# One set of expert weight buffers up to tile 63 and two from tile 64 on, where it was two from tile 34 on

## The chip, the cores and the metric

The kernel runs on one core of one Trainium2 chip. The metric is the device time of one execution in microseconds (us). TensorE (PE) multiplies, VectorE (DVE), ScalarE (ACT) and GpSimd (POOL) do the rest, and SyncE (SP) issues nearly all DMA transfers, in the order of its own queue.

## The reference

Eight sequences of 5696 tokens with 128 features are convolved along the sequence with one filter, and each token then goes through one of eight experts.

```
Xf = np.fft.rfft(x, n=2*S, axis=1); Hf = np.fft.rfft(h, n=2*S, axis=0)
y = np.fft.irfft(Xf * Hf[None], n=2*S, axis=1)[:, :S, :]
logits = y @ w_gate                      # 45568 tokens, 8 experts
expert_idx = argmax(logits); gate_w = softmax(logits)[expert_idx]
for e in range(8):                       # w1: 128x1024, w2: 1024x128
    out[mask_e] = gate_w * (relu(y[mask_e] @ w1[e]) @ w2[e])
```

## The kernel before

The convolution is three stages of matrix products over frequencies: A (lines 305 to 400, `pa`), B (`phase_b`, `xp` and `vp`) and C (`phase_c`, `yp`, which also makes the logits and scatters each token's row into `SR`, sorted by expert). The eight sequences go through them in three groups of 2, 3 and 3. While group 1 is in stage C, group 2's stage A runs beside it, and then group 2's stage B alone.

The experts are worked off in tiles of 256 sorted tokens, 185 in all. Each tile reads its first row and its expert from a small table (`tables`, line 1183). The tiles come in four parts, each of which is sorted by expert from the start: tiles 0 to 25, 26 to 58, 59 to 103 and 104 to 184. `pipeline` (line 1507) places the tiles between the work of the convolution. A tile has four steps k = 0 to 3. In step k, `layer1` makes two blocks of 128 hidden features (`mh`, lines 1375 to 1379), `relu` leaves them in `hs`, and `layer2` adds them up (`ma`, lines 1417 to 1422) two steps later. So layer 2 of a tile's steps 2 and 3 runs beside the next tile's steps 0 and 1. Up to tile 21 the tiles use plain weights; from tile 22 on, weights and activations are split into two parts and each product takes three passes.

A set of split weights is four buffers of 512 KB, `wb{z}_{n}`. Chunk n = 0 serves layer 1 of steps 0 and 1, chunk 1 of steps 2 and 3, chunks 2 and 3 serve layer 2 likewise. `load_w(t, n)` (line 1320) issues the load of chunk n of tile t from `WD`. The load carries a flag from the table: where it is 0, the transfer is skipped, as the buffer already holds that expert. It is not conditional for the first `sets(t)` tiles of a part (one, or two from part 2 on), and for two tiles that are named.

`home(t)` says which set a tile uses. It is the same set for all tiles below `LONE`, and from there on the sets 0 and 1 take turns. `user[t]` is the tile that used the set of tile t last. `pipeline` places the load of chunk n only when that tile's last step with chunk n has been placed (lines 1517 to 1524):

```
while nw[0] < min(t + 3, hi) and known(nw[0]) and (not nw[0] or state["brief"] > 3):
    was, n = user[nw[0]], nw[1]
    ...
    if was is not None and was >= lo and passed.get((was, n // 2), -1) < 2 * (n % 2) + 1:
        break
    load_w(nw[0], n)
```

SP waits at such a load until TensorE has done that step, and everything behind it in SP's queue waits as well: token rows (`xr`), matrices (`mt`), filter (`hh`) and input (`uq`) of stage B, and its output (`VU<-vt`). The table's flag compares a tile's expert with that of the tile before (`back` 1) as long as there is one set, and with that of two tiles before (`back` 2) where there are two (lines 1254 to 1258).

Of the kernel before, what the change touches and what calls it, by code (L numbers as in the profile page):

```python
# [59 lines left out]
KNOWN = (0, 2840, 2840)  # L60
STAGED = 64
PAIRED = 2
LONE = 34
HEAD = (0, 8, 2)
REST = (4, 1, 4)
FRONT = (1, 8, 2)
# [24 lines left out]
def conv_moe(ctx: ExitStack, tc: tile.TileContext, I, out, B, S, D, E, F, split):  # L91
# [1091 lines left out]
    def tables(pt, base):  # L1183
# [69 lines left out]
        nc.vector.memset(tab[:, 2, :], 1)  # L1253
        alone = min(max(LONE + 2 - sum(p.nt for p in parts[:g]), 0), NT)
        for back, lo, hi in ((1, 1, alone), (2, max(2, alone), NT)):
# [42 lines left out]
    def sets(t):  # L1298
        return 2 if seq[t][0].s >= PAIRED else 1

    def home(t):
        return (t - LONE) % 2 if t >= LONE else 0

# [16 lines left out]
    def load_w(t, n):  # L1320
        pt, j = seq[t]
        z, fixed = home(t), j < sets(t) or t in (PLAIN, LONE + 1)
        if n == 0:
# [417 lines left out]
```

## Time and profile before

| what | value |
|---|---|
| time, median of 3 runs (lowest, highest) | 2053.92 us (2049.94, 2055.18) |
| the profiled execution: its own time, span | 2054.73 us, 2053.1 us |
| TensorE busy in the span | 1975.3 us (96%) |
| DVE, ACT, POOL busy | 68%, 49%, 59% |
| weight loads `wb<-WD` on SP, moved and skipped together | 640, 512 KB each |

The span is from the first instruction to the last; the execution's own time has 1.6 us more around it. A busy share says little by itself here: the stages have different limits, and a wait is read in the stretch in which it stands.

### The profile page before, as it was taken

The numbers are of one execution on the slowest core, as the hardware profiler recorded it, in microseconds if no ns is written. First come the engines' busy times: TensorE is split into PE (matmuls) and PEld (weight loads), VectorE is DVE, ScalarE is ACT, GpSimd is POOL, SyncE is SP. The second block draws the span as 40 slices with busy tenths as digits, with TensorE's granted clock in tenths as the row PEclk, the third lists the DMA queues.
The fourth block names the chain that finished last, engine by engine and source line by source line (L and its number), as shares of the span: only waits on it lengthen the run. The fifth ranks groups of instructions, "written<-read, shape, count | busy, mean of one in ns | idle before, by whom it ended". The sixth has DMA issues, their size and how long they took to land.

```text
span 2053.1 us, 46737 instructions
## 1 busy us (share of the span) xinstructions
PE 1975.3 (96%) x14480; PEld 1517.0 (74%) x14480; DVE 1394.1 (68%) x3116; ACT 1014.6 (49%) x2219; POOL 1208.7 (59%) x1367
## 2 busy tenths in 40 slices
PE   9999898999999898989999999999999999999998
PEld 5788454555556565666766678888899999999997
DVE  6788676345644688767777666888866666666665
ACT  4788453344434454534444444444445555555554
POOL 2356177656653388885666661888875444444433
PEclk9999999999999999989999999999999999999999
DMA  9899997999998878789999987767654444443331
GB/s 361 265 295 316 320 383 289 245 278 334 303 305 296 292 265 316 254 235 289 306 296 315 297 253 250 238 202 247 214 170 156 147 148 144 149 133 122 114 102 35
DMA packets 263787, 496.80 MB, mean 242 GB/s; under 512 B 32946, under 2 KB 168887, under 8 KB 263536
## 3 DMA queue, kind: packets, MB, share of 16 engines
q1 hardware_dynamic: 239168, 445.48, 68.8%
q0 software_dynamic: 24368, 48.29, 7.1%
q8 instruction: 118, 1.93, 0.4%
q14 instruction: 133, 1.09, 0.2%
HBM read 558.54 MB, written 191.22 MB: 365 GB/s over the span
## 4 chain that ended last, share of the span: by engine, by line
PE 61%; DMA 7%; issue 4%; POOL 3%; DVE 1%; SPq 1%; ACT 1%; POOLq 0%; DVEq 0%; ACTq 0%
PE mh L1379 20%; PE ma L1422 9%; PE ma L1419 6%; PE xp L595 6%; PE ma L1417 3%; PE mx L213 3%; PE yp L896 3%; DMA wb<-WD 2%; PE mh L1376 2%; PE ma L1409 2%; PE pa L341 2%; DMA wf<-moe_w 2%; PE tp L213 2%; PE vp L666 2%; POOL SR L800 1%
## 5 line engine op out<-in xcount | busy, mean ns | idle before, releaser
L1392 DVE SCALAR_TENSOR_TENSOR hs<-mh,hs 128x512 fp32r<-128x512 f32 x640 | 440.7, 689 | 326.8 <-ACT hs L1390 326.5
L1379 PE MATMUL mh<-xtb,wb 128*128 128x256 f32 x3840 | 591.8, 290 | 15.4 <-DMA wb<-WD 10.8
L1379 PEld LDWEIGHTS mh<-xtb,wb 128*128 128x128 f32 x3840 | 519.0, 190 | 113.5 <-issue 40.0
L1390 ACT ACTIVATE hs<-mh 128x512 fp32r<-128x512 f32 x640 | 381.7, 596 | 369.2 <-PE mh L1379 346.3
L800 POOL DMA_INDIRECT SR<-rt,pi x384 | 398.1, 1037 | 217.8 <-issue 43.5
L1483 POOL DMA_INDIRECT out<-xr x264 | 258.8, 980 | 329.5 <-DVE xr L1446 277.0
L1422 PE MATMUL ma<-hs,wb 128*128 128x256 f32 x1848 | 279.6, 288 | 2.9 <-DMA wb<-WD 2.9
L705 ACT COPY vt<-vp 128x384 f32<-128x384 f32 (+1 forms) x300 | 149.9, 500 | 237.4 <-PE vp L666 226.0
L1419 PE MATMUL ma<-hs,wb 128*128 128x512 f32 x664 | 259.8, 408 | 0.0
L1422 PEld LDWEIGHTS ma<-hs,wb 128*128 128x128 f32 x1848 | 244.3, 193 | 3.7 <-DMA wb<-WD 3.5
L595 PE MATMUL xp<-uq,mt 48*64 48x384 f32 x960 | 200.8, 510 | 4.9 <-DMA uq<-VU 4.7
L666 PE MATMUL vp<-zt,mt 48*64 48x384 f32 x960 | 200.6, 509 | 0.0
L1417 PE MATMUL ma<-hs,wb 128*128 128x256 f32 x664 | 173.5, 282 | 0.0
L1483 POOL DMA_INDIRECT out<-xb x100 | 97.9, 979 | 121.6 <-ACT hs L1390 96.2
L640 DVE TENSOR_TENSOR zt<-xp,hh 128x384 f32<-128x384 f32 x240 | 122.3, 551 | 65.3 <-PE vp L666 51.0
L1419 PEld LDWEIGHTS ma<-hs,wb 128*128 128x128 f32 x664 | 125.7, 189 | 10.7 <-DVE hs L1392 0.2
L648 POOL TENSOR_TENSOR zt<-zt,hh 128x384 f32<-128x384 f32 x114 | 113.1, 1023 | 30.0 <-DVE hh L634 29.5
L1417 PEld LDWEIGHTS ma<-hs,wb 128*128 128x128 f32 x664 | 126.6, 191 | 3.5
L648 POOL TENSOR_TENSOR zt<-zt,xs 128x384 f32<-128x384 f32 x116 | 116.1, 1032 | 19.8 <-DVE xs L634 19.3
L794 POOL TENSOR_TENSOR idle_row<-idle_row 128x64 f32<-128x64 f32 (+1 forms) x288 | 117.0, 406 | 2.3
L884 DVE TENSOR_TENSOR vr<-vq 120x384 f32<-120x384 f32 x192 | 108.4, 607 | 0.0
L652 POOL TENSOR_TENSOR zt<-zt,xs 128x512 f32<-128x512 f32 x60 | 76.0, 1276 | 46.6 <-DVE xs L620 30.1
(167 smaller groups left out, 3095.6 us busy)
## 6 DMA issues: line engine op xcount, KB each, us to landing
wb<-WD SPq DMA_DIRECT2D x640, 512.0 KB
vq<-VU SPq DMA_DIRECT2D x124, 384.0 KB
VU<-vt SPq DMA_DIRECT2D x60, 768.0 KB
VU<-ut SPq DMA_DIRECT2D x48, 768.0 KB
uq<-VU SPq DMA_DIRECT2D x120, 288.0 KB
xt<-x SPq DMA_DIRECT2D x96, 256.0 KB
xr<-SR SPq DMA_DIRECT2D x182, 130.0 KB
wf<-moe_w SPq DMA_DIRECT2D x88, 256.0 KB
```

Source lines behind the costliest of these rows:

```text
L595: nc.tensor.matmul(xp[e * HP : (e + 1) * HP, :cw], lhs, uq[at, j], start=True, stop=True)
L648: eng.tensor_tensor(out=zt, in0=zt, in1=xs, op=ALU.add)
L666: nc.tensor.matmul(vp[to, :cw], mt[at, lo : lo + HP], zj, start=True, stop=True)
L705: nc.scalar.copy(dst, banks.pop(n)[:upto, : QW * cw].rearrange("p (j x) -> p j x", x=cw))
L800: s = nc.gpsimd.indirect_dma_start(out=SR[:, :], out_offset=IndirectOffsetOnAxis(ap=pi[:, b : b + 1], axis=0), in_=rt[:, b, :], in_offset= ...
L1379: nc.tensor.matmul(hp[:, u, :], wb[:, a, f, :], xt[:, b, :], start=(n == 0), stop=(n == 2))
L1390: done = nc.scalar.activation(hs[:, 0], hp, AF.Relu)
L1392: nc.vector.scalar_tensor_tensor(out=hs[:, 1], in0=hp, scalar=0.0, in1=hs[:, 0].bitcast(F32), op0=ALU.max, op1=ALU.subtract)
L1417: nc.tensor.matmul(accs[t][:, 0], wb[:, 1, f, :], hs[:, 0, u, :], start=False, stop=False)
L1419: nc.tensor.matmul(accs[t], wb[:, 0, f, :], hs[:, :, u, :], start=begin, stop=end)
L1422: nc.tensor.matmul(accs[t], wb[:, a, f, :], hs[:, b, u, :], start=(k == 0 and u == 0 and n == 0), stop=(k == NPAIR - 1 and u == 1 and n == 2),
L1483: sc = nc.gpsimd.indirect_dma_start(out=out[:, :], out_offset=IndirectOffsetOnAxis(ap=xr[:, s, D + 1 : D + 2].bitcast(I32), axis=0), in_=x ...
```

## The change

The constant `LONE` is 64 where it was 34. Three lines read it: the table's flags (1254), `home` (1302) and the tile whose load is not conditional because it fills set 1 for the first time (1322; it was tile 35, it is now tile 65).

```
-LONE = 34
+LONE = 64
...
 alone = min(max(LONE + 2 - sum(p.nt for p in parts[:g]), 0), NT)
...
 def home(t):
     return (t - LONE) % 2 if t >= LONE else 0
...
 z, fixed = home(t), j < sets(t) or t in (PLAIN, LONE + 1)
```

The order of all instructions on TensorE, ACT and POOL stays as it was; only the names of the weight buffers change. On DVE the comparisons that make the flags cover other columns of the table. Here is TensorE's queue at the end of tile 37 and the start of tile 38, in the middle of group 2's stage B (`mh37_3` is layer 1 of tile 37's step 3, `ma37` its layer 2, `wb1_1` is chunk 1 of set 1; `mh38_0` is the start of tile 38). Before:

```order
L1379 MATMUL mh37_3_12376<-xtb37_12195,wb1_1_11786 128x256 x6
L1422 MATMUL ma37_12346<-hs37_1_12304,wb1_2_11788 128x256 x6
...
L1379 MATMUL mh38_0_12420<-xtb38_12369,wb0_0_7686 128x256 x6
L1422 MATMUL ma37_12346<-hs37_2_12366,wb1_3_11790 128x256 x6
...
L1379 MATMUL mh38_1_12455<-xtb38_12369,wb0_0_7686 128x256 x6
L1422 MATMUL ma37_12346<-hs37_3_12401,wb1_3_11790 128x256 x6
```

And in the changed kernel:

```order
L1379 MATMUL mh37_3_12359<-xtb37_12178,wb0_1_7688 128x256 x6
L1422 MATMUL ma37_12329<-hs37_1_12287,wb0_2_7690 128x256 x6
...
L1379 MATMUL mh38_0_12403<-xtb38_12352,wb0_0_7686 128x256 x6
L1422 MATMUL ma37_12329<-hs37_2_12349,wb0_3_7692 128x256 x6
...
L1379 MATMUL mh38_1_12438<-xtb38_12352,wb0_0_7686 128x256 x6
L1422 MATMUL ma37_12329<-hs37_3_12384,wb0_3_7692 128x256 x6
```

The rows stand in the same places; tile 37 now reads the buffers that tile 38 reads.

On SP the weight loads keep their places too, but each place now serves one tile earlier. This is SP's queue while TensorE is in tile 36 (`xr40` are tile 40's token rows, the other transfers belong to stage B). Before, where the first row is the last chunk of tile 37 and the next four loads are tile 38's:

```order
L1340 DMA wb1_3_11790<-WD_74 128x1024
...
L1340 DMA wb0_0_7686<-WD_74 128x1024
L692 DMA VU2_72<-vt2_4_11959 128x4x384
...
L1340 DMA wb0_1_7688<-WD_74 128x1024
...
L1340 DMA wb0_2_7690<-WD_74 128x1024
...
L1313 DMA xr40_12244<-SR_69 128x260
L512 DMA mt2_28_12259<-mm 128x400
L541 DMA hh1_98<-HS_73 128x512
L530 DMA uq2_28_12262<-VU2_72 48x4x384 x2
...
L1340 DMA wb0_3_7692<-WD_74 128x1024
```

And in the changed kernel, where the first row is the last chunk of tile 36 and the next four loads are tile 37's:

```order
L1340 DMA wb0_3_7692<-WD_74 128x1024
...
L1340 DMA wb0_0_7686<-WD_74 128x1024
L692 DMA VU2_72<-vt2_4_11942 128x4x384
...
L1340 DMA wb0_1_7688<-WD_74 128x1024
...
L1340 DMA wb0_2_7690<-WD_74 128x1024
...
L1313 DMA xr40_12227<-SR_69 128x260
L512 DMA mt2_28_12242<-mm 128x400
L541 DMA hh1_98<-HS_73 128x512
L530 DMA uq2_28_12245<-VU2_72 48x4x384 x2
...
L1340 DMA wb0_3_7692<-WD_74 128x1024
```

The four loads of a tile are now issued while the tile directly before it is worked on, where it was the tile before that one. At the end of the changed stretch the shift of one tile is made up for. While TensorE is in tiles 63 and 64, SP's queue was, with the last chunk of tile 65 and then tile 66's first:

```order
L1313 DMA xr67_16843<-SR_69 128x260
...
L1340 DMA wb1_3_11790<-WD_74 128x1024
L1324 TENSOR_LOAD tab2_11702
...
L1325 TENSOR_LOAD tab2_11702
...
L1340 DMA wb0_0_7686<-WD_74 128x1024
L692 DMA VU2_72<-vt2_116_16743 128x4x384
```

In the changed kernel the first load here is the last chunk of tile 64, all four chunks of tile 65 follow, and then tile 66's first:

```order
L1313 DMA xr67_16826<-SR_69 128x260
...
L1340 DMA wb0_3_7692<-WD_74 128x1024
L1324 TENSOR_LOAD tab2_11701
...
L1340 DMA wb1_0_16876<-WD_74 128x1024
...
L1340 DMA wb1_1_16878<-WD_74 128x1024
...
L1340 DMA wb1_2_16880<-WD_74 128x1024
...
L1340 DMA wb1_3_16882<-WD_74 128x1024
L1324 TENSOR_LOAD tab2_11701
...
L1340 DMA wb0_0_7686<-WD_74 128x1024
L692 DMA VU2_72<-vt2_116_16726 128x4x384
```

Four loads that stood behind tile 34's before (tile 35's, the first filling of set 1) stand here now.

## Rows read from the trace of the kernel before

**Rows 1.** Stretches: us, busy time by engine (instructions), granted clock, DMA share, GB/s.

```profile
930.00:1240.00 310.00, 303.65 (x2465) 216.90 (x2465) 216.66 (x404) 145.85 (x296) 196.83 (x201) 0.99 0.98 293
1240.00:1540.00 300.00, 297.55 (x2833) 263.36 (x2832) 234.56 (x650) 144.41 (x377) 221.33 (x302) 1.00 0.68 217
```

**Rows 2.** Waits of PE from 930 to 1240: waiter, releaser, us, times, longest.

```profile
PE ma L1422 <- DMA wb<-WD: 2.9, 3, 1.4
PE mh L1379 <- DMA wb<-WD: 2.7, 2, 2.1
PE mh L1379 <- DVE zt L640: 0.7, 1, 0.7
```

**Rows 3.** Timeline of PE, ends of waits at tiles 34, 35, 55: start us, us, instruction.

```profile
914.05 1.62 PE L1379 MATMUL mh<-xtb,wb 128*128 128x256 f32 x6 [8.15 <-DMA wb<-WD]
...
927.85 0.99 PE L1379 MATMUL mh<-xtb,wb 128*128 128x256 f32 x6 [1.67 <-DVE zt L648]
...
1139.19 0.95 PE L1379 MATMUL mh<-xtb,wb 128*128 128x256 f32 x6 [2.15 <-DMA wb<-WD]
```

**Rows 4.** Stretches right after the waits of Rows 3.

```profile
908.20:918.30 10.10, 4.25 (x20) 2.94 (x20) 4.45 (x16) 0.60 (x1) 8.87 (x15) 0.50 1.01 303
928.70:931.90 3.20, 3.20 (x16) 1.79 (x16) 0.95 (x2) 0.80 (x2) 1.31 (x2) 0.50 0.97 334
1140.30:1143.60 3.30, 3.30 (x17) 1.89 (x16) 1.45 (x3) 0.96 (x2) 0.00 (x0) 0.50 1.04 407
```

**Rows 5.** Timeline of SP: last chunk of tile 37, chunks 0, 1, 3 of 38, 39's first.

```profile
943.64 0.09 SPq L1340 DMA_DIRECT2D wb<-WD  x1
...
945.19 0.37 SPq L1340 DMA_DIRECT2D wb<-WD  x1
...
948.22 0.34 SPq L1340 DMA_DIRECT2D wb<-WD  x1
...
953.80 0.36 SPq L1340 DMA_DIRECT2D wb<-WD  x1
...
955.63 0.36 SPq L1340 DMA_DIRECT2D wb<-WD  x1
```

**Rows 6.** Timeline of PE: starts of tiles 36, 37, 38; 38's step 2; 38's chunk 3.

```profile
939.48 0.98 PE L1379 MATMUL mh<-xtb,wb 128*128 128x256 f32 x6
...
949.64 0.98 PE L1379 MATMUL mh<-xtb,wb 128*128 128x256 f32 x6
...
959.80 0.98 PE L1379 MATMUL mh<-xtb,wb 128*128 128x256 f32 x6
...
964.67 0.98 PE L1379 MATMUL mh<-xtb,wb 128*128 128x256 f32 x6
...
970.79 0.88 PE L1422 MATMUL ma<-hs,wb 128*128 128x256 f32 x6
```

**Rows 7.** Timeline of SP: first chunks of tiles 34 and 55.

```profile
909.20 0.37 SPq L1340 DMA_DIRECT2D wb<-WD  x1
...
1128.93 0.36 SPq L1340 DMA_DIRECT2D wb<-WD  x1
```

**Rows 8.** Timeline of SP: transfers of stage B that were held.

```profile
963.04 0.33 SPq L541 DMA_DIRECT2D hh<-HS  x1
964.79 0.82 SPq L530 DMA_DIRECT2D uq<-VU  x2
```

**Rows 9.** Waits of SP from 962 to 966.

```profile
SPq L530 <- DMA wb<-WD: 1.4, 1, 1.4
...
SPq L541 <- DMA wb<-WD: 0.8, 1, 0.8
```

**Rows 10.** Timeline of PE: starts of tiles 63 and 65.

```profile
1222.67 0.98 PE L1379 MATMUL mh<-xtb,wb 128*128 128x256 f32 x6
...
1239.07 0.88 PE L1379 MATMUL mh<-xtb,wb 128*128 128x256 f32 x6
```

**Rows 11.** Timeline of SP: first chunk of tile 66, the place of tile 65's then.

```profile
1237.78 0.09 SPq L1340 DMA_DIRECT2D wb<-WD  x1
```

More of the change, by code (lines that the diff above doesn't have):

```diff
@@ L62 @@
 PAIRED = 2
-LONE = 34
+LONE = 64
 HEAD = (0, 8, 2)
```

## The prediction

> **What bounds the kernel now.** I read the stretches first, then TensorE's waits, then the queue of SP. From 930 to 1240 us, where tiles 36 to 64 run beside group 2's stage B, TensorE is busy for 303.65 of 310 us and the DMA engines for 0.98 of the time; from 1240 to 1540 TensorE is busy for 297.55 of 300 us [rows 1]. So TensorE sets the end, and what it loses before 1240 is not won back later: a wait there costs its whole length. In the changed stretch nearly all that it loses is waits for expert weights: 2.9 + 2.7 us, and 0.7 us put down to a VectorE instruction, which I count in, since it stands at the first product of tile 51 with a load outstanding: 6.3 us [rows 2]. One wait comes before it, 1.67 us at tile 35 [rows 3]. That row too names VectorE; I count it as the weights', since tile 35's own four loads stand right in front of it, behind tile 34's last in SP's queue. After a wait the granted clock can fall to 0.50, 1.2 of 2.4 GHz: it does for 3.2 us after tile 35's wait, for 3.3 us after one of 2.15 us at tile 55, and for 10.1 us around the 8.15 us at tile 34 [rows 3, 4].
>
> Which loads move data is seen on SP: a skipped load's issue takes about 0.09 us, one that moves data 0.33 or more [rows 5]. By this, among tiles 35 to 65 those of tiles 35, 38, 39, 42, 43, 46, 47, 50, 51, 54, 55, 59, 60, 64 and 65 move data, 15 of 31 tiles. An expert has about four tiles, and each of the two sets is filled with it.
>
> **What goes.** Tile 35 has tile 34's expert, so its load is skipped now; so are those of 39, 43, 47, 51 and 55, the second filling for each expert. These six tiles are 6 x 4 x 512 KB = 12.6 MB, about 14% of what 310 us at 293 GB/s move [rows 1]. Four of the six came late: the waits of rows 2 stand at tiles 47, 51 and 55, two each, for their first and their last chunk, and the one before is tile 35's. With them go 6.3 + 1.67 us of waiting, and the half-speed stretches behind tiles 35 and 55, which cost half their length: 1.6 + 1.65 us. Sum of the gain: 11.2 us. It cannot be much more, as TensorE has no other idle time in this stretch.
>
> **What comes: an expert's first tile.** The loads keep their places in SP's queue but now serve one tile earlier, so a load that had two tiles' time has one. Tile 38 shows the places [rows 5, 6]. Its chunk 0 is issued 945.19 - 939.48 = 5.71 us after the start of the tile in which it is issued. Now that is tile 37, and tile 38 starts 10.16 us after it (949.64 - 939.48, the next is 10.16 too). How long a chunk takes from issue to use is shown only where someone waits. The shortest is 914.05 - 909.20 = 4.85 us at tile 34, which already uses one set and whose loads stand behind skipped ones; the longest is 1139.19 - 1128.93 = 10.26 us at tile 55, behind another tile's four loads [rows 3, 7]. From 4.85 us the wait is 0.4 us, from 10.26 it is 5.8; I take 0.4, since now skipped loads stand ahead. Chunk 1 is issued at 948.22 - 939.48 = 8.74 us and wanted at 964.67 - 949.64 = 15.03 us after tile 37's start, which leaves 6.3 us: no wait.
>
> Chunk 3 is worse. It is issued 953.80 - 939.48 = 14.32 us after that start, as it waits for layer 2 of the tile before, and is wanted by layer 2 at 970.79 - 949.64 = 21.15 us: 6.8 us. It has the transfers of stage B directly ahead of it, and still will. Its landing is seen: the `hh` transfer at 963.04 is the eighth after it and was held for a weight load, so it took 963.04 - 953.80 = 9.2 us [rows 5, 8, 9]. The wait is 2.4 us. The bounds are none (from 4.85 us) and 3.4 us (from 10.26).
>
> So a change of expert costs 0.4 + 2.4 = 2.8 us, and there are five at which no second load follows (tiles 38, 42, 46, 50, 54): 14.0 us. Waits of 1.67 and 2.15 us were followed by half speed; 2.4 us is longer, but it is one wait per tile and I take three of five, 3 x 1.65 = 5.0 us.
>
> **Tiles 59 and 60.** Both are the first of part 2 and load without condition. With two sets this filled both. Now tile 60 fills the one set a second time with the same expert, and has to wait for it. Tile 59's chunk 0 costs 0.4 us. Tile 60's chunk 0 stands where tile 39's stood, 955.63 - 949.64 = 5.99 us after the start of the tile before, right behind that tile's chunk 3. There it took 964.79 - 955.63 = 9.2 us [rows 5, 8, 9]; 15.15 - 10.16 gives a wait of 5.0 us. Tile 60's chunk 3 costs 2.4 us again, and I take half speed twice, 3.3 us. Sum of the two tiles: 11.1 us. Bounds for tile 60: 0.7 us (all loads 4.85 us) and 16 us (10.26 us, chunk 3 at 3.4, and the 5 us of half speed that tile 34 shows).
>
> **Tiles 64 and 65.** Tile 64 is a change of expert in the one set, 0.4 us at its start. Tile 65 then fills set 1 for the first time, in the place in which the first chunk of tile 66 stood: 1237.78 - 1222.67 = 15.1 us after tile 63's start, while tile 65 starts 16.4 us after it [rows 10, 11]. From 4.85 us the wait is 3.6 us, from 9.2 it is 7.9. I take 3.6 us, since stage B's transfers have ended by then, and one half-speed stretch: together 5.6 us. What tile 64's last chunk adds lies under this wait.
>
> **Everything else** costs nothing: TensorE's order is the same, two small flag comparisons on VectorE change their width, and SP's waits at the weight loads are for the same steps of TensorE as before, so what is queued behind them is not later than TensorE itself.
>
> **Sum.** 14.0 + 5.0 + 11.1 + 5.6 = 35.7 us lost, 11.2 us won: 24.5 us longer. The profiled execution took 2054.73 us, 1.6 us of it around its span, which gives 2079.2; the median of the runs is 0.8 us below that execution, so I predict 2078.4 us.
>
> **The rivals.**
>
> *The loads land in time, and the time falls.* The point from which this decides is 4.45 us for a chunk 0 (10.16 - 5.71) and 6.8 us for a chunk 3. For it speaks that 12.6 MB of traffic go, and that the queue is emptier at each change. Then only tile 65 waits, 15.1 + 4.45 - 16.4 = 3.2 us, and the time is 11.2 - 3.2 = 8 us shorter, 2046 us. Against it speaks that no wait shows a chunk in under 4.85 us, and chunk 3's neighbours in the queue stay. The Trainium skill, DMA: Bandwidth & Descriptors, section "Anatomy of one DMA", counts about 2.0 us fixed and the bytes at 436 GB/s for one transfer; it is measured for GpSimd's queue. For 512 KB that would be 3.2 us, an estimate by that page; by it no expert's first tile would wait and this rival would hold. The trace does not agree: 4.85 to 10.26 us, since a transfer here shares the engines with others.
>
> *Gain and loss cancel.* With chunks that land in 4.85 us everywhere the losses are 5 x 0.4 + 0.4 + 0.7 + 0.4 + 3.6 = 7.1 us without half speed: 4 us shorter, 2050 us; with chunk 3 at 8 us (1.2 us each at six places) it is 3 us longer, 2057.
>
> *Each change costs what tile 34 costs.* There TensorE waited 8.15 us for a single set, in this same stage, and lost 5 us more at half speed [rows 3, 4]. At seven places (38, 42, 46, 50, 54, 59, 60) this is 92 us; with tile 65's 5.6 less 11.2 it makes 2140 us. Against it: tile 34's first load was issued at 909.20, 3.3 us after TensorE had begun to wait for it (914.05 - 8.15 = 905.9), as stage B had only begun and SP was late [rows 3, 7]; later a chunk 0 is issued 4.45 us before its tile can start [rows 5, 6].
>
> *The change doesn't do what it says* I leave out: the queue shows the names of one set, and the flags compare with the right tile.
>
> **How the numbers follow.** Forecast 0.70; in time and faster 0.08; cancel 0.16; like tile 34 at each change 0.06. A measurement of this kernel can tell 0.3%, 6 us, from no change. Faster by more than that is the first rival, with 0.07 of its 0.08. Within it are the second, 0.16, and the rest of the first: 0.17. Slower: 0.76. The forecast's own range goes from 2065 (chunk 3 at 8 us, and half speed at tiles 60 and 65 alone) to 2110, where chunk 0 takes 7.5 us, halfway between the bounds, and chunk 3 takes 10.26. To leave out no more than 2 in 10 I take 2052 to 2104.
>
> **What would show it.** After the change: TensorE's busy time in the stretch of stage B stays near 304 us and the stretch becomes some 20 us longer; waits of `mh` and `ma` for `wb` at every expert's first tile and the one behind it, the longest at tile 60, and another at 65; none at 47, 51, 55; a DMA share well under 0.98; the stretch behind tile 66 as long as before. I am wrong if chunk 3 lands within 6.8 us of its issue, if tile 60 doesn't wait, or if the tiles between changes become faster than 10.16 us.

## The result, and the profile after

| | before | after |
|---|---|---|
| median of 4 runs each, same chip | 2051.93 us | 2075.06 us |
| lowest to highest | 2049.92 to 2055.18 | 2068.22 to 2079.07 |
| profiled execution, span | 2054.73, 2053.1 | 2079.07, 2077.3 |
| start of tile 34 to start of tile 66 | 331.2 us | 354.5 us |
| start of tile 66 to the end of the last matmul | 801.8 us | 801.5 us |

The ratio is 1.0106, with an interval of 1.0083 to 1.0128: the changed kernel is slower by 17 to 26 us. The two last rows, read from TensorE's timeline, say where. The spans differ by 24.2 us; 23.3 us of it lie between tile 34 and tile 66, and what follows is as long as it was.

The same stretches as in [rows 1], after the change (us, busy time by engine with instructions, granted clock, DMA share, GB/s):

```profile
930.00:1264.00 334.00, 313.44 (x2459) 222.71 (x2460) 217.19 (x405) 145.86 (x295) 198.15 (x202) 0.96 0.83 239
...
1269.90:1569.90 300.00, 297.56 (x2826) 263.17 (x2825) 234.93 (x651) 144.07 (x376) 223.41 (x304) 1.00 0.67 214
```

The same work takes 334 us where it took 310. TensorE has some 20 us without work in it, where it had 6, and its busy time is 10 us longer at as many instructions, since the granted clock is 0.96 on average and was 0.99. The DMA share fell from 0.98 to 0.83: the page counts 484.21 MB where it counted 496.80, 12.6 MB less, as worked out. Fewer bytes, and yet more waiting.

SP's own waits show how both go together (for SP: waiter, releaser, us, times, longest). Before, from 930 to 1240 us, SP was held mostly by transfers that had not landed (the first row and others like it, over 70 us in all), and less by TensorE's steps (the other two):

```profile
SPq L1340 <- DMA VU<-vt: 18.3, 17, 1.6
...
SPq L1340 <- PE mh L1379: 9.8, 9, 2.1
SPq L1340 <- PE ma L1422: 8.9, 9, 3.2
```

After, from 930 to 1264 us, it is the other way round:

```profile
SPq L1340 <- PE ma L1422: 52.5, 43, 8.3
SPq L1340 <- PE mh L1379: 49.3, 29, 2.6
SPq L1340 <- DMA VU<-vt: 6.2, 6, 1.3
```

Landings now hold it for under 18 us, and it spends 101.8 us waiting until TensorE is done with the one set. Here are TensorE's waits of that stretch (waiter, releaser, us, times, longest), against [rows 2]:

```profile
PE ma L1422 <- DMA wb<-WD: 12.8, 8, 3.2
PE mh L1379 <- DMA wb<-WD: 7.6, 4, 4.9
```

And the instructions at which the longer ones end, from TensorE's timeline (start, us, instruction, in brackets the wait before it):

```profile
972.18 1.19 PE L1422 MATMUL ma<-hs,wb 128*128 128x256 f32 x6 [1.80 <-DMA wb<-WD]
...
1010.78 0.98 PE L1422 MATMUL ma<-hs,wb 128*128 128x256 f32 x6 [1.03 <-DMA wb<-WD]
...
1017.65 0.98 PE L1422 MATMUL ma<-hs,wb 128*128 128x256 f32 x6 [1.75 <-DMA wb<-WD]
...
1061.17 1.17 PE L1422 MATMUL ma<-hs,wb 128*128 128x256 f32 x5 [2.60 <-DMA wb<-WD]
...
1106.91 1.44 PE L1422 MATMUL ma<-hs,wb 128*128 128x256 f32 x5 [3.18 <-DMA wb<-WD]
...
1152.89 1.02 PE L1422 MATMUL ma<-hs,wb 128*128 128x256 f32 x6 [1.77 <-DMA wb<-WD]
...
1209.93 1.41 PE L1379 MATMUL mh<-xtb,wb 128*128 128x256 f32 x5 [4.91 <-DMA wb<-WD]
...
1257.59 0.95 PE L1379 MATMUL mh<-xtb,wb 128*128 128x256 f32 x6 [1.65 <-DMA wb<-WD]
...
1263.68 0.95 PE L1379 MATMUL mh<-xtb,wb 128*128 128x256 f32 x6 [0.62 <-DMA wb<-WD]
```

The rows at 972, 1017, 1061, 1106 and 1152 us are chunk 3 of the five experts that begin at tiles 38, 42, 46, 50 and 54, one each, in the tile behind. The row at 1010 is chunk 2 of tile 42. Then come the start of tile 60, chunk 1 of tile 64 (4.79 us into that tile) and the start of tile 65. The rest of the loss is the clock. These are the stretches behind four of the waits (columns as above):

```profile
972.90:976.10 3.20, 3.20 (x17) 1.79 (x16) 1.02 (x2) 0.48 (x1) 0.00 (x0) 0.50 1.07 275
1017.70:1020.90 3.20, 3.20 (x26) 2.43 (x26) 1.02 (x2) 1.00 (x2) 0.00 (x0) 1.00 0.97 267
1106.00:1112.60 6.60, 5.69 (x26) 4.28 (x26) 1.33 (x3) 1.08 (x2) 0.06 (x1) 0.50 0.80 205
1208.40:1215.00 6.60, 5.07 (x23) 3.69 (x24) 1.26 (x3) 1.08 (x2) 0.00 (x0) 0.50 0.73 287
```

Three have a granted clock of 0.50, 1.2 of 2.4 GHz: 17 matmuls in 3.2 us, where the second row, at full clock, has 26. In all six stretches at 0.50 stand in the changed part, 27.2 us long, so 13.6 us lost at half their length. About 1.2 us of this is counted twice, as TensorE is busy for only 5.69 and 5.07 us of the two long rows: the clock fell while it still waited. TensorE's busy time confirms the half: of the 27.2 us, 2.4 lie in these waits, and 5.2 us at 0.50 stood in this stretch before [rows 4]; half of the 19.6 us left is 9.8 us, by which the busy time grew.

### The profile page after: what moved, and what is told of

It is laid out like the page before. It is cut to its first block, busy times and chain, and to the rows that moved or that the text cites. A ratio compares the mean times of both kernels' runs of the same rounds, so it can differ in the third digit from the quotient of the medians.

```text
span 2077.3 us, 46684 instructions
## 1 busy us (share of the span) xinstructions
PE 1982.7 (95%) x14480; PEld 1522.4 (73%) x14480; DVE 1393.6 (67%) x3116; ACT 1016.2 (49%) x2219; POOL 1209.6 (58%) x1367
## 2 busy tenths in 40 slices
DMA packets 260332, 484.21 MB, mean 233 GB/s; under 512 B 32563, under 2 KB 168504, under 8 KB 260081
## 4 chain that ended last, share of the span: by engine, by line
PE 60%; DMA 7%; issue 4%; POOL 4%; DVE 1%; SPq 1%; ACT 1%; POOLq 0%; DVEq 0%; ACTq 0%
PE mh L1379 20%; PE ma L1422 9%; PE ma L1419 6%; PE xp L595 6%; DMA wb<-WD 4%; PE ma L1417 3%; PE mx L213 3%; PE mh L1376 3%; PE yp L896 3%; PE ma L1409 2%; POOL SR L800 2%; PE pa L341 2%; PE vp L666 2%; PE tp L213 1%; POOL out L1483 1%
## 5 line engine op out<-in xcount | busy, mean ns | idle before, releaser
L1422 PE MATMUL ma<-hs,wb 128*128 128x256 f32 x1848 | 282.1, 289 | 12.9 <-DMA wb<-WD 12.8
L1419 PEld LDWEIGHTS ma<-hs,wb 128*128 128x128 f32 x664 | 125.6, 189 | 10.8 <-DVE hs L1392 0.2
```

The source lines that it names most:

```text
L1419: nc.tensor.matmul(accs[t], wb[:, 0, f, :], hs[:, :, u, :], start=begin, stop=end)
L1422: nc.tensor.matmul(accs[t], wb[:, a, f, :], hs[:, b, u, :], start=(k == 0 and u == 0 and n == 0), stop=(k == NPAIR - 1 and u == 1 and n == 2),
```

## Experiments

Chips differ: the kernel before took 2052 to 2055 us in three of the five groups of runs and 2095 and 2109 us in two, so each time, a median, stands beside that of the kernel before on the same chip. The ratio is an estimate from all executions, with its 95% interval in brackets, and need not equal the quotient of the two medians. "Stretch" is the time from tile 34's start to tile 66's in the one profiled execution; it was 331.2 us before. The changed kernel was run twice, with 354.5 and 351.1 us, so a difference of 3 us between two stretches shows little by itself.

### The changed kernel once more

No edit. It ran on one chip with the three repeats below.

> The changed kernel once more, beside the next three on one chip (the two calls before had chips on which the kernel before takes 2053 and 2109 us). Theory (the cost is in the stretch of the one set and does not depend on the rest): 1.010 to 1.013 of the kernel before on the same chip, tile 34's to tile 66's start 352 to 357 us. Rival (it depends on the chip): outside these.

Measured: 2072.17 against 2054.73 us, ratio 1.0089 (1.0067 to 1.0112), stretch 351.1 us. Ratio and stretch both lie just under the ranges expected, so the expectation missed by its own words; the interval overlaps the first one. TensorE's waits for weights:

```profile
PE ma L1422 <- DMA wb<-WD: 10.8, 6, 2.9
PE mh L1379 <- DMA wb<-WD: 8.8, 4, 4.6
```

The sum is 19.6 us where it was 20.4. The result stands; 17 to 23 us lies in both intervals.

### Tile 60 skips its load

In the changed kernel tile 60 loads without condition, though tile 59 has just filled the same set with the same expert. Here its flag decides.

```
-return 2 if seq[t][0].s >= PAIRED else 1
+return 2 if seq[t][0].s >= PAIRED and t >= LONE else 1
```

> The changed kernel, but tile 60's load carries its flag, so that it is skipped (same expert as tile 59). Theory (tile 60 pays for filling the one set a second time): its wait of 4.9 us and the 6.8 us at half speed behind it (3.4 us lost) go, and tile 59's chunk 3 now waits at tile 60 as it does at the other changes (about 2.2 us and 1.7 us of half speed): 4.4 us less than the changed kernel's 2075.1, 2070.7 us. Rival (the start of a part costs this whatever tile 60 loads, by the rows of its table and the queue): no change, 2075 us.

Measured: 2072.67 against 2053.11 us, ratio 1.0082 (1.0056 to 1.0108), stretch 350.7 us. As a time this is not told apart from the changed kernel. As a row it is: tile 60 starts without a wait, and what waits in it is layer 2 for tile 59's own chunk 3 (TensorE's timeline).

```profile
1203.86 1.44 PE L1422 MATMUL ma<-hs,wb 128*128 128x256 f32 x5 [2.46 <-DMA wb<-WD]
```

The wait of 4.91 us became one of 2.46, and 6.8 us at 0.50 still follow it. So tile 60's second load costs about 2.5 us of waiting: without it, tile 59's chunk 3, which it covered, comes out.

### Two sets from tile 59 on

Tile 60 then fills a set of its own, while nothing else changes between 34 and 58.

```
-LONE = 64
+LONE = 59
```

> LONE = 59: one set up to tile 58, two from 59 on, so tile 60 fills set 1 for the first time and tiles 64 and 65 are as before the change. Theory: tile 60's wait and half speed go (4.9 + 3.4 us), those of tiles 64 and 65 too (1.65 + 0.62 + 1.7 us), tile 59's chunk 3 waits instead (about 2.2 + 1.7 us): 8.4 us less than the changed kernel, 2066.7 us; the five changes of expert between 38 and 54 keep their cost. Rival (whichever tile fills set 1 first pays, since its four loads come behind the last chunk of the tile before): tile 60 waits 3 to 5 us and the time is 2071 to 2073 us.

Measured: 2072.84 against 2053.11 us, ratio 1.0075 (1.0052 to 1.0099), stretch 354.1 us. The theory fell and the rival held; only the waits at tiles 64 and 65 went as the theory said. TensorE's row at tile 60's start:

```profile
1208.96 1.62 PE L1379 MATMUL mh<-xtb,wb 128*128 128x256 f32 x6 [4.80 <-DMA wb<-WD]
```

And SP's row of the load that it waits for, tile 60's chunk 0:

```profile
1198.86 0.36 SPq L1340 DMA_DIRECT2D wb<-WD  x1
```

In the changed kernel the same load was issued at 1200.10 us; in both it is 5.3 us after tile 59's start. A free buffer doesn't bring it earlier, as it stands behind tile 59's chunk 3 in SP's queue. The place in the queue makes tile 60 wait, not the buffer.

### The two sets take turns by expert

If the loss is that a change of expert has no free set, then two sets that change places at each expert's first tile should remove it, and the gain of the skipped second loads should stay. Tile 60 skips its load here too, and tile 64, a new expert as well, takes the set that is free.

```
+SWITCH = (38, 42, 46, 50, 54, 59)
+SWITCHING = (0, 1, 2, 3)
...
+def home(t, n):
+    if t >= LONE:
+        return (t - LONE + SWITCHED) % 2
+    return sum(t >= s for s in SWITCH) % 2 if n in SWITCHING else 0
...
+fixed = whole or t in SWITCH and n in SWITCHING
...
```

> Two sets that take turns by expert and not by tile: the set changes at tiles 38, 42, 46, 50, 54 and 59 (loaded there without condition), at 64 and then from tile to tile; the second filling is still gone and the four loads of a new expert wait for no tile of the old one. Theory (the change wins 11.2 us by the loads that go and pays with waits for the one set): the waits of both kernels go, 2051.9 - 11.2 = 2040.7 us, and no wait for wb of over 1 us stands at tiles 38 to 65. Rival 1 (the second loads cost nothing, the waits of before only move to stage B's own transfers): 2050 to 2053 us. Rival 2 (four loads at once are late for their first chunk, as SP places them only 5.9 us ahead): waits of 1 to 3 us at each change, 2047 to 2055 us.

Measured: 2047.14 against 2053.11 us, ratio 0.9958 (0.9941 to 0.9975), stretch 321.2 us. The waits are as the theory had them: none for weights is over 0.5 us from tile 38 to tile 65. The time is 6 us above its 2040.7 us and, taken alone, would also fit the second rival, whose waits of 1 to 3 us are not there. The profiled execution, 2040.10 us, was the fastest of twelve. It was run again:

> The sets that take turns by expert (e3_by_expert) once more on this chip: 0.994 to 0.998 of the kernel before by the first chip; tile 34's to tile 66's start 320 to 324 us. Rival: on this chip it is the same as before (0.999 to 1.001), as other waits come first.

Measured: 2043.13 against 2054.73 us, ratio 0.9946 (0.9928 to 0.9964), stretch 320.4 us; on the same chip the changed kernel took 2072.17. TensorE's waits from 920 to 1236 us, in the repeat:

```profile
PE mh L1387 <- DMA wb<-WD: 1.3, 2, 0.9
```

And the stretch of stage B (columns as above):

```profile
930.00:1235.00 305.00, 303.73 (x2491) 219.28 (x2490) 217.95 (x406) 147.84 (x300) 197.92 (x202) 1.00 0.88 259
```

1.3 us of waits are left of 20, and the clock is 1.00 throughout. TensorE's busy time is that of [rows 1] again. The stretch is 10 to 11 us shorter than before the change, nearly the 11.2 us that the prediction counted as the gain. So the gain is there; the changed kernel gives it away, and more, mostly at the changes of expert.

### A second buffer for chunk 3 alone

The same code, with only chunk 3 changing its buffer: 512 KB more than the changed kernel uses there, not 2 MB.

```
+SWITCHING = (3,)
+SWITCHED = 0
```

> The changed kernel with a second buffer for chunk 3 alone, used by turns from expert to expert between tiles 38 and 63; chunks 0 to 2 keep one buffer. Theory (at a change of expert TensorE waits for chunk 3, because its load is issued only after the layer 2 of the tile before): the waits of 1.80, 1.75, 2.60, 3.18 and 1.77 us (11.1) and the half speed behind them (17 us, 8.5 lost) go, tiles 60, 64 and 65 stay: 19.6 us less than 2075.1, 2055.5 us. Rival (the transfers are slow whenever they are issued, as stage B fills the DMA engines): the waits move to chunk 2, 1 to 2 us each with half speed behind some: 2065 to 2072 us.

Measured: 2053.30 against 2053.11 us, ratio 0.9996 (0.9974 to 1.0019), stretch 336.4 us. TensorE's waits from 930 to 1256 us:

```profile
PE mh L1387 <- DMA wb<-WD: 9.7, 7, 3.7
```

No row of `ma` is left: layer 2 waits nowhere. Tile 38's chunk 3 is now issued 0.6 us before the tile's start and no longer 4.25 us after it. One buffer takes 15 to 18 us of the stretch away, by the two runs of the changed kernel; the profiled execution, 2064.10 us, lies 10.8 us above the median, so its stretch may be a long one. What is left is mostly at the starts of tiles 59 (1.03 us), 60 (3.68) and 65 (2.99) and in tile 64 (0.98), so the term of chunk 3 is shown to be the largest by far. With tile 60's flag as well (the two edits together):

> The changed kernel with a second buffer for chunk 3 alone (e5_chunk3) and tile 60's load carrying its flag (e1_flag60), so one more buffer of 512 KB instead of four up to tile 63. Theory (between tiles 38 and 63 the one set costs only by chunk 3 and by tile 60's load): of e5_chunk3's stretch, 336.4 us from tile 34's to tile 66's start, tile 60's wait of 3.7 us and 3.4 us of half speed go: 329 us; 0.996 to 0.998 of the kernel before on the same chip. Rival (chunks 0 to 2 are late as well once tile 60 doesn't let the queue run empty, or tile 59's loads then make tile 60 wait): 334 us or more and no faster than the kernel before.

Measured: 2091.01 against 2095.21 us, ratio 0.998 (0.9962 to 0.9997), stretch 329.5 us, at a chunk's price in buffers; 1.85 us before tile 50's start and 1.6 and 2.2 us in tile 64 and at tile 65 are the longest waits that it leaves.

### The traffic of the second loads without their waits

The kernel by expert, and at tiles 39, 43, 47, 51 and 55 the second loads are put back, into the set that nobody reads. Their traffic returns, and nobody waits for them.

```
 nc.sync.dma_start(dst, WD[n, ds(ew, P), :], **kw)
+if t in EXTRA:
+    free = wbuf[1 - z, n].bitcast(F32).rearrange("p a c f -> p (a c f)")
+    nc.sync.dma_start(free, WD[n, ds(ew, P), :])
```

> The kernel whose sets take turns by expert (e3_by_expert), with the traffic of the second fillings put back: at tiles 39, 43, 47, 51 and 55 the four chunks are loaded once more, into the set that is free, where nobody waits for them. Theory (the change won because TensorE waited for the second loads themselves): the time stays near e3's 2047 us, at most 3 us more, and from tile 34's to tile 66's start it is 321 to 325 us. Rival (the change won because the DMA engines were full): stage B's own transfers or the next expert's loads come late instead, and the stretch goes back to about 331 us, the time to 2053 us.

Measured: 2114.46 against 2109.25 us, ratio 1.0033 (1.0016 to 1.0049), stretch 337.2 us. The theory that only a load that is waited for costs something fell. With a new one the kernel was run again beside the kernel by expert:

> The traffic put back (e4_traffic) once more, on the chip of e3b. New theory (traffic costs by itself, since tiles that skip their load still wait until SP's queue has come to the skipped load): 10 to 16 us more than e3b, waits of 1 to 4 us for wb at the tiles behind 39, 43, 47 and 51, which load nothing. Old theory (only a load that is waited for costs): within 3 us of e3b; the 14 us that e4_traffic's stretch was longer were the other chip.

Measured: 2057.32 against 2054.73 us, ratio 1.0017 (0.9997 to 1.0037), stretch 333.3 us: 14.2 us over the kernel by expert on the same chip, 12.9 in the stretch. The size is as expected; the place only in part. TensorE's timeline:

```profile
980.74 1.09 PE L1391 MATMUL mh<-xtb,wb 128*128 128x256 f32 x6 [1.78 <-DMA wb<-WD]
...
1047.01 1.20 PE L1391 MATMUL mh<-xtb,wb 128*128 128x256 f32 x4 [2.52 <-DMA wb<-WD]
...
1133.56 0.95 PE L1391 MATMUL mh<-xtb,wb 128*128 128x256 f32 x6 [1.44 <-DMA wb<-WD]
```

Tiles 46 (1047) and 54 (1133) are first tiles of an expert: their own loads come late. Tile 40 (980) skips its load, and still waits. SP's timeline shows for what:

```profile
970.41 0.34 SPq L1352 DMA_DIRECT2D wb<-WD  x1
...
978.22 0.09 SPq L1349 DMA_DIRECT2D wb<-WD  x1
978.51 0.36 SPq L1352 DMA_DIRECT2D wb<-WD  x1
980.54 0.08 SPq L1349 DMA_DIRECT2D wb<-WD  x1
```

The last row is tile 40's first load, skipped in 0.08 us, and the product starts 0.2 us after it. A skipped load moves nothing, but its reader waits until SP has come to it. The extra loads take SP 0.34 and 0.36 us each to issue, and they hold it longer by their landing. These are SP's waits for weight loads at stage B's input, in this kernel from 930 to 1250 us and, below, in the kernel by expert from 930 to 1235:

```profile
SPq L534 <- DMA wb<-WD: 10.6, 12, 2.0
```

```profile
SPq L533 <- DMA wb<-WD: 5.5, 8, 1.3
```

So a load that nobody needs costs by itself, even where nobody waits for its bytes: it holds the queue and delays the loads that are needed. How much of the 12.9 us goes by each of the two is not shown.

### A switch at tile 34 too

```
+SWITCH = (34, 38, 42, 46, 50, 54, 59)
```

> The kernel whose sets take turns by expert, from tile 34 on (a switch at 34 as well, so tile 34 fills set 1 without waiting for a step of tile 33). Theory (tile 34's wait of 8 to 10 us comes of SP being late at the start of stage B, not of the one set): the wait of tile 34 stays between 7 and 10 us, the time near 2047 us. Rival (it is the one set that makes tile 34 wait, as at the later changes): the wait falls under 2 us and with it the 10 us at half speed, 2034 us.

A single execution: 2100.97 us where the kernel before took 2109.25, stretch 322.7 us. TensorE's row at tile 34:

```profile
951.39 1.62 PE L1387 MATMUL mh<-xtb,wb 128*128 128x256 f32 x6 [8.41 <-DMA wb<-WD]
```

The wait at tile 34 is as long as in [rows 3], with a set that no tile was using, so the one set does not make it. What makes SP late there is seen in the kernel before: from 896 to 910 us it waited 7.4 us for stage B's `uq`, `mt` and `hh` to land, and for no step of TensorE.

### The wait of chunk 3 filled with products

Of the 34.0 us lost, 13.6 are put down to the clock. Here TensorE does layer 1 of the first step of tiles 39, 43, 47, 51 and 55 four times (18 more products), so that it works instead of waiting. The last of the four counts.

```
-layer1(t, k)
+layer1(t, k, 4 if k == 0 and t - 1 in FILLED else 1)
```

> The changed kernel, with TensorE kept busy where it waits for chunk 3: at the start of tiles 39, 43, 47, 51 and 55 layer 1's six products are done four times into the same bank, 18 more products (about 2.5 us) in front of the layer 2 that waits; the result is the same. Theory (of what the change costs, 8.5 us are half speed behind these five waits of 2.2 us): the waits of layer 2 there fall under 0.7 us, the clock stays at full speed, and 8.5 us less 5 x 0.3 us are won: 2068 us, and tile 34's to tile 66's start falls from 354.5 to about 348 us. Rival (the clock falls anyway, or what is lost behind a wait is the wait alone): the extra products come on top, 2 us more than the changed kernel, 2077 us.

Measured: 2123.82 against 2109.25 us, ratio 1.0071 (1.0048 to 1.0094), stretch 348.4 us; there was no run of the changed kernel on that chip to set it against. So both were run on one chip:

> The waits for chunk 3 filled with products (e7_fill), on the chip of after2. Theory (half speed behind these waits costs 8.5 us and is saved): 4 to 9 us less than after2, stretch from tile 34's to tile 66's start 346 to 350 us. Rival (what is lost is the wait alone): as after2 or 2 us more.

Measured: 2065.84 us, ratio 1.0054 (1.0034 to 1.0074), against 2072.17 and 1.0089 (1.0067 to 1.0112) for the changed kernel: 6.3 us less, with intervals that just overlap, and 3.2 us less in the stretch. TensorE's stretch in the filled kernel and, below, in the changed one of that chip:

```profile
930.00:1258.00 328.00, 316.73 (x2545) 230.18 (x2544) 213.94 (x398) 145.61 (x295) 195.32 (x198) 0.98 0.84 244
```

```profile
930.00:1264.00 334.00, 314.40 (x2485) 226.80 (x2484) 217.57 (x406) 147.32 (x298) 197.69 (x202) 0.96 0.83 242
```

And the waits that the filled kernel still has:

```profile
PE mh L1380 <- DMA wb<-WD: 7.8, 6, 3.1
PE ma L1423 <- DMA wb<-WD: 3.2, 4, 1.6
```

The filled step of tile 39 on TensorE's timeline (the others took as long), where the six products took 0.98 us:

```profile
962.71 3.14 PE L1380 MATMUL mh<-xtb,wb 128*128 128x256 f32 x24
```

Five times 2.16 us, 10.8 us of work without use, replace 8.6 us of waits (19.6 less 11.0), which alone would make it 2.2 us longer. But the granted clock is 0.98 where it was 0.96, and the time at 0.50 falls from 23.9 to 10.2 us, which is 6.8 us less lost; at the five filled places none of it is left, where 13.7 us stood. The sum is 4.6 us shorter; the stretch shows 3.2 and the medians 6.3. So the half speed behind a wait is a cost of its own, as counted, though the intervals leave its size open.

## Why the prediction was right, and where its terms were off

The direction, the mechanism and the size came out as forecast: 2075.06 against 2078.4 us. Lost were 20.4 us of waits and 13.6 at half speed, 34.0 where 35.7 was worked out; less the 11.2 us won this is 22.8 us, and the stretch grew by 23.3. By its steps:

| step | forecast | measured |
|---|---|---|
| waits at 35, 47, 51, 55 and their half speed go | 11.2 | gone (by expert: 10.0 and 10.8 us won) |
| chunk 0 at five changes | 2.0 | 0 |
| chunk 3 at five changes | 12.0 | 11.1 |
| chunk 2 of tiles 42 and 54 | 0 | 1.5 |
| tile 59's and tile 60's waits | 7.8 | 5.35 |
| tiles 64 and 65 | 4.0 | 2.4 |
| half speed in all | 9.95 | 13.6 |

**Right.** TensorE sets the end, and behind tile 66 nothing was won back. Chunk 3 is the large term: mean wait 2.2 us for 2.4. Its landing was read off rightly as well. Here is SP's row of tile 38's chunk 3:

```profile
963.04 0.36 SPq L1340 DMA_DIRECT2D wb<-WD  x1
```

Its product ran at 972.18 us, 9.1 us later (9.3 to 10.3 us at the other four changes); 9.2 was read from a transfer that had been held behind it [rows 5, 8]. The second buffer for chunk 3 alone shows that it is this chunk's place, and not the bytes of all four.

**Held, but not reasoned.** The prediction read the places in time at tile 38 alone and used them at all five changes. In the kernel before they did not last: chunk 0 was issued 14.6 us before tile 38's start, and only 8.1, 7.7 and 8.0 us before those of tiles 46, 50 and 54, as SP fell behind, held by transfers. After the change it is issued 4.4 to 4.5 us before each of the five. Here is SP's row of tile 46's chunk 0, before (the tile starts at 1041.13 us) and, below, after (1047.42 us):

```profile
1033.06 0.37 SPq L1340 DMA_DIRECT2D wb<-WD  x1
```

```profile
1042.98 0.37 SPq L1340 DMA_DIRECT2D wb<-WD  x1
```

One tile's time, 10.16 us, leaves 4.4 of 14.6 us and nothing of 8.1: had SP stayed that late, the waits would, by the prediction's own sums, have been longer. The prediction said that SP's waits are for the same steps of TensorE as before; in fact those steps set SP's pace only after the change. That tile 38's places then held everywhere was luck as far as its working goes.

**Off in size.** Chunk 0 was given 0.4 us per change from the shortest landing in the trace, 4.85 us. Of the first tiles only tile 59 waited so, 0.44 us: where skipped loads stand ahead, a chunk 0 landed within the 4.45 us that it has (in the repeat tile 50 waited 0.45 us). This was the point from which the first rival decides, and for chunk 0 that rival held. Half speed was counted at three of five changes and one stretch of 3.3 us each. It stood behind four of the five waits for chunk 3, and behind the two longest waits (3.18 and 4.91 us) it was 6.8 us long. Tile 65 waited 0.62 us for 3.6 (2.47 in the repeat), and tile 64 had a wait for chunk 1 of 1.65 that wasn't foreseen. With 0.16 us more in tile 64 that is 2.4 for 4.0. One sign was wrong: TensorE's busy time in the stretch was to stay near 304 us and is 313.4; the 9.95 us at half speed that the prediction itself counted had to show there. Two bounds are not the sums of their terms: tile 60's 16 us comes to 14.5 (6.1, 3.4 and 5), and the 2110 us to about 2106.

**Right number, half of the reason.** The 5.0 us at tile 60 came out as 4.91. The prediction said that tile 60 "fills the one set a second time with the same expert", and has to wait for it. The second filling is needed: where it is skipped, tile 60 starts without a wait. The one set is not: with a set of its own tile 60 waited 4.80 us. What counts is that its first load is queued behind tile 59's chunk 3, which was in the working of the number, and not in the reason. Tile 60's own chunk 3, given 2.4 us, didn't wait: it was issued at 1216.4 us, behind the wait, and by then the DMA engines had run empty (their share is 0.06 in this stretch, columns as in [rows 1]), so one wait paid for the next.

```profile
1213.00:1216.40 3.40, 3.40 (x24) 2.08 (x24) 1.14 (x3) 1.11 (x3) 0.00 (x0) 0.69 0.06 21
```

Waits in one chain were added where the earlier covers the later; with tile 60's load skipped another covered one, tile 59's chunk 3, appears, 2.46 us.

**Incomplete.** The gain was said to be the waits for the second loads and their half speed. The size is right, but with those loads back and nobody waiting for them 12.9 us of the stretch were lost again, at the next expert's first tiles and at tile 40. The second loads cost through the transfers and the queue places that they push back, though before, the waits stood at their own products.

**Open.** Why the clock fell behind the wait of 1.80 us and not behind that of 1.75 is not settled: in the repeat it fell behind 1.92 us there and not behind 2.12 us at tile 55. Nor does the length follow the wait: in the repeat 6.8 us at 0.50 stood behind a wait of 2.58 us and 3.4 behind one of 2.92.

## What to carry to other kernels

When a buffer set is taken away, ask for each load how long it now has from the moment its old reader is done to the first product that needs it, chunk by chunk, and compare that with landings read in the same stretch: here one chunk of four lacked 2.2 us on average at each change, and the others nearly always had time. The cure is a second buffer where the change of data is, not for everything: two sets that take turns by expert save the traffic and the wait, 29 us under the changed kernel on the same chip, and one more buffer for the late chunk alone makes the changed kernel as fast as the one before. Look also at what the issuing queue itself waits for: places read where transfers hold it move when traffic goes. A stall of TensorE costs its length and often a stretch at half clock behind it, here 20 us and 12 to 14 us.

## What the runs showed of the hardware

A load of 512 KB took at most 4.5 us (chunk 0, behind skipped loads) and 9.1 us (chunk 3, behind the expert's other chunks and stage B's transfers) at one and the same change of expert, tile 38: at the same size, so the difference lies in what else was queued. A skipped load takes 0.08 to 0.09 us of SP's time and still holds its reader until SP has come to it: 1.78 us at tile 40. With waits of 1.65 to 4.9 us came stretches of 3.4 or 6.8 us at a granted clock of 0.50, or none (1.75 us, and 2.12 in the repeat).
